# A quarter of two gradient stores moved to GpSimd's queue and spread unevenly over the DMA engines

## The chip, the cores and the metric

The kernel runs on one core of a Trainium2 chip. The core has a matrix engine (TensorE, "PE" in the profile, with its weight loads as "PEld"), VectorE ("DVE"), ScalarE ("ACT"), GpSimd ("POOL") and SyncE ("SP", which here only issues transfers). Transfers are carried out by 16 DMA engines. The metric is the device time of one execution in microseconds (us). The kernel before takes 638.99 us, the median of 3 runs (638.45 to 639.02).

## The reference

One query row per head attends to 8192 keys, for 32 heads of 128 columns, in bf16. The outputs are the attention result and the gradients of q, k and v for a given gradient of the output:

```python
scores = jnp.einsum('bhqd,bhkd->bhqk', q, k) * scale
attn = softmax(scores)
out = jnp.einsum('bhqk,bhkd->bhqd', attn, v)
# and the vjp of it: dq, dk, dv for grad_out
```

With one query row, dV is the outer product of attn and grad_out, and dK the outer product of the score gradient and q. K and V are read once (67 MB each) and dK and dV written once (67 MB each); everything else is small. K, V, dK and dV are [1, 32, 8192, 128].

## The kernel before

The 32 heads are taken as 16 pairs. A pair's K (or V, dK, dV) is a tile of 128 partitions with 128 rows of 128 bf16 numbers each, so 32 KB a partition and 4 MB in all. K tiles have 3 buffers, V tiles 2. `outer` writes dK and dV into the very tiles that held K and V, and the tiles are stored from there. A tile is worked on in 8 slices `r` of 16 rows (`NU` = 8).

Window j of the main loop (L328) does, for pair j, the scores from K, the softmax, the transposes of V (`v_transposes`, L202), the result (`contract` with "p") and dV (`outer`, L270); between them it finishes pair j-1: the score gradient, dQ (`contract` with "ds") and dK (`outer`, L270). The order of instructions on each engine is written out by hand (`tc.manual_schedule`), so what the program lists first is issued first.

All large transfers are issued from SP, in program order, and each of the 16 DMA engines works through its part of them in that order. In the steady windows SP issues, once each: the store of dK of pair j-1 (L278), the load of V of pair j+1 (`load_v`, L90, which waits until dV of pair j-1 has left that buffer), the store of dV of pair j (L278) and the load of K of pair j+2 (`load_k`, L84, which waits until dK of pair j-1 has left its buffer). Each is 4 MB in 128 packets of 32 KB, eight for each DMA engine. The first four pairs store in halves; the last pairs store in halves and quarters (`PARTS`), and the last V comes in quarters.

From window 6 on, `mark` (L104) issues one tiny load after each load of V or K, 15 in all: the n-th takes 4 bytes for each of n partitions into a small tile that nothing reads.

GpSimd does some memsets and the identity at the start, and nothing afterwards.

Of the kernel before, what the change touches and what calls it, by code (L numbers as in the profile page):

```python
# [11 lines left out]
BF16 = mybir.dt.bfloat16  # L12
# [10 lines left out]
K_BUFS = 3  # L23
V_BUFS = 2
QD = 32


@with_exitstack
def kernel(
# [11 lines left out]
    nc = tc.nc  # L41
    P = 128
# [4 lines left out]
    NT = 2 * S // P  # L47
    NU = NT // CH
    NQ = P // QD
    assert NU == 8 and NQ == 4  # L50
    W = D // 2
    NB = W // QD
    NG = NT // 4
# [3 lines left out]
    consts = ctx.enter_context(tc.tile_pool(name="consts", bufs=1))  # L57
# [12 lines left out]
    Kt, Vt, XK, XV, st, acc, qd = {}, {}, {}, {}, {}, {}, {}  # L70

    def rows_of(x, j, c=0, parts=1):
        L = NT // parts
        return x[0, 2 * j:2 * j + 2].rearrange("b s d -> (b s) d").rearrange("(p n) d -> p n d", p=P)[:, c * L:(c + 1) * L, :]

    def slots(X, c, parts):
        L = NT // parts
        return X[:, c * L:(c + 1) * L, :]

    def load_k(j):  # L80
        Kt[j] = kpool.tile([P, NT, D], BF16, tag="K", name="Kt")
        parts = 4 if j == 0 else 1
        for c in range(parts):
            nc.sync.dma_start(slots(Kt[j], c, parts), rows_of(k, j, c, parts))  # L84

    def load_v(j):
        Vt[j] = vpool.tile([P, NT, D], BF16, tag="V", name="Vt")
        parts = 4 if j in (0, HP - 1) else 1
        for c in range(parts):
            nc.sync.dma_start(slots(Vt[j], c, parts), rows_of(v, j, c, parts))  # L90
# [3 lines left out]
    nc.scalar.dma_start(rows[:, 1, :], grad_out.rearrange("b h s d -> (b h s) d"))  # L94
    load_k(0)
    load_v(0)
    load_k(1)
    load_v(1)
    load_k(2)

    marks = list(range(1, 16))
    marked = consts.tile([16, len(marks), 2], BF16)

    def mark():  # L104
        n = marks.pop(0)
        nc.sync.dma_start(marked[0:n, n - 1], k[0, 0].rearrange("(p n) d -> p n d", p=P)[0:n, 0, 0:2])

    ident = consts.tile([P, P], BF16)
    make_identity(nc, ident[:])
# [9 lines left out]
    nc.gpsimd.memset(q_win[:], 0.0)  # L119
    do_win = consts.tile([P, 2, 2, QD + 8], BF16)  # L120
    nc.gpsimd.memset(do_win[:], 0.0)
    wins = {}
    for which in ("p", "ds"):
        wins[which] = consts.tile([P, NG, QD], BF16, name=f"win_{which}")
        nc.gpsimd.memset(wins[which][:], 0.0)
# [3 lines left out]
    q_blk = consts.tile([P, HP, 2 * NB, NQ], BF16)  # L129
    four = small.tile([H, 2 * NB, NQ, QD], BF16, tag="S", name="four")  # L130
    for w in range(NB):
        for e2 in range(2):
            nc.scalar.copy(
                four[:, 2 * w + e2], rows[:, 0, :].rearrange("h (w j e) -> h w e j", w=NB, e=2)[:, w, e2:e2 + 1, :]
                .to_broadcast([H, NQ, QD]))
    tp = psT.tile([P, 2 * TB, P], BF16, tag="T", name="tp_q")
    for c in range(2 * NB):
        nc.tensor.transpose(tp[:, c, 0:H], four[:, c].rearrange("h a j -> h (a j)"), ident[0:H, 0:H])
    lane = consts.tile([P, QD], F32)
# [126 lines left out]
    def outer(j, which, r):  # L266
        x = st[j]
        G, dst = (Kt[j], out_2) if which == "dk" else (Vt[j], out_3)
        rep, row = x["ds"] if which == "dk" else x["p"], qd[j][:, 0 if which == "dk" else 1, :]
        nc.vector.tensor_tensor(  # L270
            slots(G, r, NU).rearrange("p n (a b) -> p n a b", b=R),
            slots(rep, r, NU).unsqueeze(2).to_broadcast([P, CH, D // R, R]),
            row.rearrange("p (a b) -> p a b", b=R).unsqueeze(1).to_broadcast([P, CH, D // R, R]),
            op=ALU.mult)
        parts = PARTS.get((which, j - HP), 2 if j < SPLIT else 1)
        if r % (NU // parts) == NU // parts - 1:
            c = r // (NU // parts)
            nc.sync.dma_start(rows_of(dst, j, c, parts), slots(G, c, parts))  # L278

# [48 lines left out]
    for j in range(HP + 1):  # L328
# [42 lines left out]
        if ends and j > 0:  # L371
            gather_copy("ds")
            if early:
                half(j, 0)
            for r in range(NU):
                outer(p_, "dk", r)
            if j + 1 < HP:
                load_v(j + 1)
# [9 lines left out]
        if not ends:  # L388
            gather_copy("ds")
            outer(p_, "dk", 0)  # L390
            outer(p_, "dk", 1)
# [44 lines left out]
        if not ends:  # L436
            for r in range(4, NU):
                outer(p_, "dk", r)
            if j + 1 < HP:
                load_v(j + 1)  # L440
                if j >= 6 and marks:
                    mark()
        for r in range(NU):
            if early:
                contract(j, "p", 4 * r, 4 * r + 4)
# [17 lines left out]
            do_window(j + 1)  # L463
        if 0 < j and j + 2 < HP:
            load_k(j + 2)
            if j >= 6 and marks:
                mark()

    result(dq_all, out_1)
    order.__exit__(None, None, None)  # L470
# [30 lines left out]
```

## Time and profile before

| | |
|---|---|
| median of 3 runs | 638.99 us (638.45 to 639.02) |
| the profiled execution | 638.61 us |
| its span, first to last instruction | 636.6 us |
| busy share of PE, DVE, ACT, POOL | 78%, 81%, 35%, 0% |
| bytes moved by DMA | 269.01 MB, 423 GB/s over the span |
| SP's queue ("q1"), share of 16 engines' time | 98.6% |

The table takes its numbers from the profile's page. The span is shorter than the time of its execution by 2.0 us, which lie before the first and after the last instruction. A queue's share says what part of the time of all 16 DMA engines its packets took. The trace has each packet's start, duration, size and queue, but not which of the 16 engines carried it.

### The profile page before, as it was taken

Reading aid. Unit: us, or ns where it says so; the run is one execution under the profiler, and the core shown is the slowest. Engines: PE = TensorE matmul, PEld = TensorE weight load, DVE = VectorE, ACT = ScalarE, POOL = GpSimd, SP = SyncE. Lnnn points to the kernel's source line nnn. Section 1 sums busy time; section 2 is a strip of 40 time slices with the busy share of each in tenths; the row PEclk is TensorE's granted clock in tenths of the full one; section 3 lists DMA queues with packets and bytes.
Section 4 is the critical chain, followed back from the end, with each engine's and each line's share of the span. In section 5 each row is a group of like instructions: output and inputs, shape, how many; then the busy total and the mean of one; then the engine's idle time right before and its main releaser. Section 6 shows DMA issues by size and latency. Waiting matters only on the chain.

```text
span 636.6 us, 8553 instructions
## 1 busy us (share of the span) xinstructions
PE 498.7 (78%) x3480; PEld 283.3 (44%) x3480; DVE 518.0 (81%) x654; ACT 221.8 (35%) x508; POOL 3.2 (0%) x10
## 2 busy tenths in 40 slices
PE   4787776888787987877978778887788877798771
PEld 1454443354453635444354453545436354363541
DVE  6589897979889798896789877798777987779882
ACT  2442434043342514335043340533405244152430
POOL 1000000000000000000000000000000000000000
PEclk9989899769798786979679797796977868779775
DMA  8999999999999999999999999999999999999995
GB/s 364 434 437 402 435 433 424 423 428 434 433 429 433 429 427 432 429 432 431 434 428 430 432 429 428 438 435 430 427 427 433 430 442 430 429 428 421 429 398 231
DMA packets 12854, 269.01 MB, mean 423 GB/s; under 512 B 1808, under 2 KB 1808, under 8 KB 1808
## 3 DMA queue, kind: packets, MB, share of 16 engines
q1 hardware_dynamic: 12720, 268.46, 98.6%
q8 instruction: 27, 0.44, 0.3%
q14 instruction: 11, 0.09, 0.0%
q10 hardware_dynamic: 96, 0.02, 0.0%
HBM read 134.23 MB, written 134.23 MB: 422 GB/s over the span
## 4 chain that ended last, share of the span: by engine, by line
PE 41%; DMA 26%; DVE 23%; ACT 4%; issue 3%; DVEq 0%; ACTq 0%; SPq 0%
DMA Kt<-in_k_dram 19%; PE s_ps L185 15%; PE T_ps L202 12%; DVE Kt L270 7%; DMA out_dram<-Kt 7%; DVE XK_sb L175 7%; PE acc_p L249 4%; PE acc_ds L249 4%; PE m_ps L262 3%; DVE Vt L270 3%; PE dp_ps L219 2%; ACT XV_sb L207 2%; DVE sT L192 1%; DVE dpT L230 1%; ACT p_rep L423 1%
## 5 line engine op out<-in xcount | busy, mean ns | idle before, releaser
L270 DVE TENSOR_TENSOR Vt<-p_rep,qd 128x2048 bf16<-128x2048 bf16 x128 | 155.4, 1225 | 55.2 <-PE acc_p L249 43.7
L185 PE MATMUL s_ps<-XK_sb,q_win 128*128 128x512 bf16 x512 | 152.3, 430 | 39.1 <-DVE XK_sb L175 33.6
L175 DVE STREAM_TRANSPOSE XK_sb<-Kt 128x1024 f32<-128x1024 f32 x128 | 151.3, 1221 | 21.1 <-PE s_ps L185 12.9
L207 ACT COPY XV_sb<-T_ps 128x512 f32<-128x512 f32 x256 | 139.9, 591 | 81.0 <-PE T_ps L202 80.9
L202 PE MATMUL T_ps<-ident_f,Vt 128*128 128x128 f32 x1024 | 167.2, 317 | 0.8 <-DMA Vt<-in_v_dram 0.8
L270 DVE TENSOR_TENSOR Kt<-ds_rep,qd 128x2048 bf16<-128x2048 bf16 x128 | 149.5, 1215 | 2.8 <-PE acc_ds L249 2.4
L202 PEld LDWEIGHTS T_ps<-ident_f,Vt 128*128 128x128 f32 x1024 | 133.7, 163 | 36.9 <-issue 20.5
L185 PEld LDWEIGHTS <-q_win 128*128 128x128 bf16 x512 | 51.5, 111 | 123.7 <-issue 92.1
L249 PE MATMUL acc_p<-Vt,win_p 128*32 128x512 bf16 x512 | 56.2, 441 | 3.3 <-ACT win_p L241 3.3
L249 PE MATMUL acc_ds<-Kt,win_ds 128*32 128x512 bf16 x512 | 42.5, 427 | 4.6 <-ACT win_ds L241 4.6
L219 PE MATMUL dp_ps<-XV_sb,do_win 128*32 128x512 bf16 x512 | 34.7, 386 | 13.5 <-ACT XV_sb L207 13.5
L255 ACT COPY S_ds<-acc_ds 128x512 f32<-128x512 f32 x16 | 9.4, 587 | 85.8 <-PE acc_ds L249 85.8
L241 ACT COPY win_ds<-ds 64x128 bf16<-64x128 bf16 x32 | 9.5, 296 | 75.6 <-DVE ds L300 75.4
L411 ACT ACTIVATE e<-sT,nbias 128x128 f32<-128x128 f32 x16 | 8.2, 515 | 69.7 <-DVE nbias L407 69.7
L262 PE MATMUL m_ps<-lane,S_ds 128*128 128x2 f32 x128 | 25.8, 324 | 4.1 <-DVE rinv L421 4.1
L219 PEld LDWEIGHTS <-do_win 128*32 128x32 bf16 x512 | 14.3, 94 | 29.3 <-issue 22.6
L262 PEld LDWEIGHTS m_ps<-lane,S_ds 128*128 128x128 f32 x128 | 24.4, 284 | 6.2 <-DVE rinv L421 5.2
L412 PE MATMUL m_ps<-rs,ones_f 128*128 128x1 f32 x32 | 8.0, 318 | 24.3 <-ACT e L411 24.3
L249 PEld LDWEIGHTS <-win_p 128*32 128x32 bf16 x512 | 13.4, 96 | 28.7 <-issue 25.5
L262 PEld LDWEIGHTS m_ps<-lane,S_p 128*128 128x128 f32 x128 | 21.4, 240 | 5.7 <-issue 2.3
L249 PEld LDWEIGHTS <-win_ds 128*32 128x32 bf16 x512 | 9.5, 100 | 32.0 <-issue 28.2
L398 PE MATMUL m_ps<-ident_f,top 128*128 128x128 f32 x16 | 4.8, 300 | 23.6 <-DVE top L396 23.6
(59 smaller groups left out, 201.3 us busy)
## 6 DMA issues: line engine op xcount, KB each, us to landing
Kt<-in_k_dram SPq DMA_DIRECT2D x15, 4096.0 KB
Vt<-in_v_dram SPq DMA_DIRECT2D x14, 4096.0 KB
out_dram<-Vt SPq DMA_DIRECT2D x11, 4096.0 KB
out_dram<-Kt SPq DMA_DIRECT2D x10, 4096.0 KB
out_dram<-Vt SPq DMA_DIRECT2D x10, 2048.0 KB
out_dram<-Kt SPq DMA_DIRECT2D x10, 2048.0 KB
Vt<-in_v_dram SPq DMA_DIRECT2D x8, 1024.0 KB
Kt<-in_k_dram SPq DMA_DIRECT2D x4, 1024.0 KB
```

Source lines behind the costliest of these rows:

```text
L175: nc.vector.transpose(XK[j, u][:].rearrange("p g w i -> p (g w i)"), slots(Kt[j], u, NU).rearrange("p g d -> p (g d)").bitcast(F32))
L185: nc.tensor.matmul(st[j]["s"][:], lhsT=q_win[:, c, at:at + P], rhs=cols[:, c // 2, c % 2], start=(u == 0 and c == 0), stop=(u == NU - 1 an ...
L202: nc.tensor.transpose(T_ps[:, i, :], words[:, m * P:(m + 1) * P], ident_f[:])
L207: nc.scalar.copy(XV[j][:, b * TB:(b + 1) * TB, :], st[j].pop(("T", c))[:])
L219: nc.tensor.matmul(out[b * QD:(b + 1) * QD, :], lhsT=do_win[:, b // 2, e2, at:at + QD], rhs=cols[:, z, e2, :, b * QD:(b + 1) * QD], start= ...
L241: nc.scalar.copy(wins[which][t * M:(t + 1) * M, :, 4 * t:4 * t + 4], src[t * M:(t + 1) * M])
L249: nc.tensor.matmul(acc[which][b * QD:(b + 1) * QD, :], lhsT=wins[which][:, g, :], rhs=X[:, 4 * g:4 * g + 4, :].rearrange("p n d -> p (n d) ...
L255: nc.scalar.copy(S[:].rearrange("p j d -> p (j d)"), acc.pop(which)[:])
L262: nc.tensor.matmul(bank[:, at:at + 2], lhsT=S[:, i, :], rhs=pick[:, i, 0:2], start=(i == 0), stop=(i == 3), skip_group_check=True)
L270: nc.vector.tensor_tensor(slots(G, r, NU).rearrange("p n (a b) -> p n a b", b=R), slots(rep, r, NU).unsqueeze(2).to_broadcast([P, CH, D // ...
L411: nc.scalar.activation(e[:].rearrange("p (u g) -> p u g", u=NU), x["sn"], ACT.Exp, bias=nbias[:], scale=scale, accum_out=rs[:])
L412: nc.tensor.matmul(x["m"][:, 0:1], lhsT=ones_f[:], rhs=rs[:], start=True, stop=True, skip_group_check=True)
```

## The change

The 15 marks are gone. For pairs 7 and 9 the store of dV is cut: SP stores the first three quarters of each partition's rows as soon as slice 5 is done, and GpSimd stores the last quarter (32 rows, 8 KB a partition, 1 MB in all) after slice 7. GpSimd does so with several transfers over groups of partitions, listed in `STEER` as (number of partitions, first DMA engine). The program assumes that a transfer over n partitions is spread over the largest divisor of n up to 16 engines, that these are consecutive, and that they start at a cursor which each transfer moves on by that number. `turn_to` moves the cursor to the wanted engine with a dummy load of as many partitions as the cursor must advance. These transfers are cut into packets of 4 KB (`max_dma_last_dim=4096`), and so is the load of V that stands in SP's queue ahead of them (pairs 8 and 10).

```diff
+SHARE = 4
+STEER = {
+    7: ((38, 15), (38, 7), (19, 2), (33, 5)),
+    9: ((98, 5), (30, 10)),
+}
     def load_v(j):
         Vt[j] = vpool.tile([P, NT, D], BF16, tag="V", name="Vt")
+        if j - 1 in STEER:
+            nc.sync.dma_start(Vt[j][:], rows_of(v, j), max_dma_last_dim=4096)
+            return
...
-    def mark():
-        n = marks.pop(0)
-        nc.sync.dma_start(marked[0:n, n - 1], k[0, 0].rearrange("(p n) d -> p n d", p=P)[0:n, 0, 0:2])
+    spare = list(range(8))
+    turned = consts.tile([16, len(spare), 2, 2], BF16)
+    cursor = [0]
+
+    def turn_to(lane):
+        n = (lane - cursor[0]) % 16
+        if n:
+            i = spare.pop()
+            nc.gpsimd.dma_start(turned[0:n, i], k[0, 0].rearrange("(p n) d -> p n d", p=P)[0:n, 0:2, 0:2])
+        cursor[0] = lane
+
+    def store_steered(dst, G, j):
+        a, c = 0, SHARE - 1
+        for n, lane in STEER[j]:
+            turn_to(lane)
+            nc.gpsimd.dma_start(rows_of(dst, j, c, SHARE)[a:a + n], slots(G, c, SHARE)[a:a + n], max_dma_last_dim=4096)
+            a += n
+            cursor[0] = (lane + max(m for m in range(1, 17) if n % m == 0)) % 16
+        assert a == P
+        if j == max(STEER):
+            turn_to(0)
...
-        if r % (NU // parts) == NU // parts - 1:
+        if which == "dv" and j in STEER:
+            L = NT - NT // SHARE
+            if r == NU - NU // SHARE - 1:
+                nc.sync.dma_start(rows_of(dst, j)[:, 0:L, :], G[:, 0:L, :])
+            elif r == NU - 1:
+                store_steered(dst, G, j)
+        elif r % (NU // parts) == NU // parts - 1:
...
-                if j >= 6 and marks:
-                    mark()
...
-            if j >= 6 and marks:
-                mark()
```

More of the change, by code (lines that the diff above doesn't have):

```diff
@@ L99 @@
     load_k(2)
-    marks = list(range(1, 16))
-    marked = consts.tile([16, len(marks), 2], BF16)
-    def mark():
-        n = marks.pop(0)
-        nc.sync.dma_start(marked[0:n, n - 1], k[0, 0].rearrange("(p n) d -> p n d", p=P)[0:n, 0, 0:2])
+    spare = list(range(8))
[17 more added lines that the diff above has]
+            turn_to(0)
     ident = consts.tile([P, P], BF16)
```

## The prediction

> **What bounds the kernel now.** I read the shares first, then the chain that ended last, SP's queue, and the end of the run. The page says that the DMA engines are full:
>
> ```profile
> DMA  8999999999999999999999999999999999999995
> DMA packets 12854, 269.01 MB, mean 423 GB/s; under 512 B 1808, under 2 KB 1808, under 8 KB 1808
> q1 hardware_dynamic: 12720, 268.46, 98.6%
> q8 instruction: 27, 0.44, 0.3%
> ```
>
> The digits are busy tenths of the 16 engines together; SP's queue alone takes 98.6% of them. In the chain, a load of K of 29 us is followed by compute and by a store of dK of 23 us, which frees the buffer for the next load:
>
> ```profile
> 349.20 29.35 DMA Kt<-in_k_dram
> ...
> 405.19 22.66 DMA out_dram<-Kt
> 427.89 29.35 DMA Kt<-in_k_dram
> ```
>
> 4 MB take an engine 8 packets of 1.213 us, 9.7 us; the other 13 to 20 us are the queue. So the loop runs at the pace of the DMA engines, and since a landing counts only when all 16 engines are through, of the slowest of them. The end shows that they are not alike (columns: stretch and length in us, four engines' and GpSimd's busy us, clock, DMA share, GB/s):
>
> ```profile
> 618.00:628.00 10.00, 3.92 (x18) 3.44 (x17) 5.98 (x6) 1.75 (x7) 0.00 (x0) 0.50 1.00 419
> 628.00:632.00 4.00, 0.00 (x0) 0.00 (x0) 0.00 (x0) 0.00 (x0) 0.00 (x0) 0.50 0.35 141
> 632.00:636.60 4.60, 0.00 (x0) 0.00 (x0) 0.00 (x0) 0.00 (x0) 0.00 (x0) 0.50 0.04 16
> ```
>
> After 628 us no compute is left and the engines drop out one by one; from 632 us on the share is 0.04, less than one engine of 16. The kernel waits for a single DMA engine.
>
> Which one, the packet records tell. On a busy engine one packet starts 3 ns before the last ends, so the packets fall into 16 chains. The marks number them: mark n leaves its 4-byte packets in n chains, each mark in one chain more than the one before. The lag of each engine behind the first, when the last 4 MB of dV and the next half of dK are through (605 us), and its end of data where that stands apart:
>
> ```
> engine   0   1   2   3   4    5   6   7   8   9   10  11  12  13  14  15
> lag us  0.0 2.0 0.1 7.0 10.8 4.3 3.8 0.0 0.1 7.6 6.2 4.8 4.6 3.9 4.0 0.1
> end us              631.7 634.9              632.3 630.9
> ```
>
> All carry the same bytes. Engines 0, 2, 7, 8 and 15 carry no instruction fetch (queues q8 and q14); the others get 3 to 6 each, a 16 KB one delaying its engine by about 1.4 us (0.95 for its packet, the rest on the data packet beside it), and engine 4's packets run slow by small amounts all along.
>
> **The change part by part.** Its core is rows per engine. A quarter of dV is 128 rows of 8 KB, 16 for each engine over the two pairs. By the divisors the diff counts on, 38 rows go to 2 engines, 19 to 1, 33 to 11, 98 to 14, 30 to 15, which makes
>
> ```
> engine       0  1  2  3  4  5  6  7  8  9 10 11 12 13 14 15
> rows after  28  9 28  2  2 12 12 31 31 10 12 12 12 12 12 31
> ```
>
> in place of 16 everywhere: most where the lag is 0, least on 3 and 4.
>
> Prices. Median packets take 1.213 us for 32 KB, 0.611 for 16 KB, 0.309 for 8 KB: about 8 ns fixed, the rest by bytes. A 4 KB packet then is (0.309+0.008)/2 = 0.1585 us, if nothing comes on top for alternating between two queues. Bounds for that extra: nothing or slightly less (ACT's 256-byte packets at the start ran between SP's at 15 to 18 ns, with SP's still at 309), and 0.34 us (a 16 KB instruction fetch took 0.95 against 0.611). I take nothing: ACT's is the row with a data queue.
>
> - Rows taken off: the 24 KB packets of the shorter store save 16 x 0.303 = 4.85 us on each engine. Rows put back: 0.317 us each (two packets).
> - V of pairs 8 and 10 in 4 KB packets: 64 x 0.1585 - 8 x 1.213 = 0.44 us, twice, 0.88 on each engine.
> - GpSimd issues 13 transfers (6 stores, 7 dummies); their completion packets, at most 15 ns each on an engine: 0.2 us. The dummies' 4-byte packets are in this.
> - Marks out: two 4-byte packets, about 13 ns each, on n engines: -0.3 us on engine 4 (11 marks), -0.15 on 9. On SP each took 0.3 us in a queue that waits anyway: nothing.
> - SP: the store of three quarters leaves two slices (2.6 us) earlier; SP waits for DVE there anyway, and the ring has 20 us of work ahead. Nothing.
> - GpSimd was idle after 4 us, so its own time costs nothing unless late (below). Order and counts on PE, DVE and ACT stay.
> - New wait: the load of V of pair 9 (and 11) waits for GpSimd's stores too; behind it in SP stand dV's store and the next K load. It was issued at 329.44 us, when the last engine had finished dV of pair 7, 328.9. Engines 7, 8 and 15 get 44 GpSimd packets beside the 64 of the V load, so the two alternate and end together, 7 us later there, at 321.9 us instead of 314.9; the three-quarter store gives 2.4 back, 329.2. Nothing. The transposes of V 8 start at 323.89, 2 us after that landing:
>
> ```profile
> 323.89 1.97 PE L202 MATMUL T_ps<-ident_f,Vt 128*128 128x128 f32 x8
> ```
>
> Sums, on the ends of data:
> engine 4: -4.85 + 0.63 + 0.88 + 0.2 - 0.3 = -3.4, from 634.9 to 631.5;
> engine 9: -4.85 + 3.17 + 0.88 + 0.2 - 0.15 = -0.75, from 632.3 to 631.6;
> engine 10: -0.1, 630.8; engine 3: 628.3;
> engines 7, 8, 15: without idling engine 0 would have ended at 632.3 - 7.6 = 624.7 (it idled 3.4 us for late issues); plus 9.83 - 4.85 + 0.88 + 0.2 = 6.1, so 630.8.
> The last end moves from 634.9 to 631.6 us, by 3.3. Compute follows: the last K load lands when engine 4 is through, lag 8.0 at 527 us; after the change the largest lag there is the 6.1 of 7, 8 and 15 (their part of the sum above), 1.9 us earlier, which is more than the last stores need, as engines 4 and 9 have work queued to the end. From the profiled 638.61 us that is 635.3. It lies 0.38 under the median and within the runs shown; from the median it would be 635.7. I say 635.5.
>
> The skill speaks against giving engines 7 and 15 the most: the Trainium skill, DMA: Bandwidth & Descriptors (Latency and other measured facts), calls them usually slower than the rest when GpSimd's descriptor rings are in use. In the trace of before, without such rings, they are among the fastest (lags 0.0 and 0.1); no row shows them with rings, and this is the second rival's mechanism.
>
> **The rivals.**
> *The rows land on other engines* (slower). The diff assumes spreading by divisor and a cursor at 0; no row shows a GpSimd transfer. If each is dealt out in equal shares over up to 16 engines from engine 0, 38 rows make 3 each, 19 make 2, 98 make 7: engines 0 to 8 get 20 rows, 13 to 15 get 9, 2 and 0. Engine 4: -4.85 + 6.34 + 0.8 = +2.3, end 637.2, time 640.9. It decides from 13 rows on engine 4, where the sum turns positive. The Trainium skill, DMA: Bandwidth & Descriptors (Why a DMA increments its semaphore), states both: the divisor with a round-robin cursor, and for some direct copies of GpSimd such equal shares. The marks, issued from SP, bear the diff's rule out below 16: their n rows went to n engines, always from the same one on. Above 16 no row tells the two apart.
>
> *GpSimd's packets cost more beside SP's.* Engines 7, 8, 15 carry 62 of them and have 634.9 - 630.8 = 4.1 us to lose: at 66 ns a packet the gain is gone, at 100 ns the time is 640.7.
>
> *The stores come late.* SP's V 9 load has until 343.5 us, when the engines run out of issued work. If GpSimd takes over 5 us for each transfer, the second store of 38 rows, third in its queue after 298.7 us, misses the V load, which is through at 315, and its packets alternate with 24 and 32 KB ones, about 1.1 us each; 38 of them end near 357 us, all engines idle some 14 us, time near 650. The Trainium skill, SBUF — State Buffer (the "DVE blocks DMA" trap), has a cause: DVE can lock GpSimd out while it writes descriptors. DVE is busy from 300.3 us, but in pieces of at most 1.25 us.
>
> *Nothing gained.* The fetches fall elsewhere: one more on 9 or 4 costs 1.4 us. Two more and the time is within 0.2%, 638.1.
>
> **How the numbers follow.** 0.2% (1.3 us) is about what a measurement here can tell from no change. Forecast 0.66, its own range 634.2 (one fetch fewer on each of 4 and 9) to 637.2 (one more). Other engines 0.12, packets 0.10 (a third of it within 0.2%), late 0.05, nothing gained 0.07. Faster 0.66, same 0.11, slower 0.23. To leave out no more than 2 in 10 the range goes up to the first rival's 640.9.
>
> **What would show it.** Right: the share after 632 us near zero and the span near 633.3; GpSimd's queue with 512 packets of 4 KB in about 20 us after 299 us; V 9 issued near 329 us, T_ps of V 8 without a wait; ends of engines within 3 us. Wrong: one engine alone draining at the end (rows misplaced), packets over 0.2 us (price), a hole in the DMA digits near 340 us (late).

## The result, and the profile after

The changed kernel takes 644.38 us (644.02 to 645.4) against 639.0 us (638.45 to 639.29): a ratio of 1.0088, with an interval of 1.007 to 1.0105. It is slower by 5.4 us, where 3.5 us less was forecast, and it lies above the range. The profiled execution took 644.35 us, its span is 642.4 us.

The page of the changed kernel, the lines on the DMA engines (digits and GB/s in 40 slices of the span, then packets and queues):

```profile
DMA  8999999999999999999997999999999999999996
GB/s 364 445 433 397 444 425 419 423 428 433 431 430 438 427 427 430 440 426 427 417 427 281 407 427 383 445 433 427 427 435 438 424 428 434 436 427 417 433 427 292
DMA packets 16934, 269.01 MB, mean 419 GB/s; under 512 B 3584, under 2 KB 3584, under 8 KB 6144
q1 hardware_dynamic: 14272, 266.36, 97.4%
q0 software_dynamic: 2528, 2.11, 1.0%
```

The digits were 9 from the second slice to the last but one; now there is a 7, in the slice that begins at 337 us, where GB/s falls to 281. GpSimd's queue, q0, holds 2528 packets. Only 512 of them are the expected 4 KB ones: the other 2016 have 4 or 8 bytes.

The stretch with the hole, by windows (columns as at the end of the kernel before: stretch and length, busy us of PE, PEld, DVE, ACT and POOL, clock, DMA share, GB/s):

```profile
342.00:346.00 4.00, 3.13 (x20) 2.02 (x20) 3.93 (x9) 0.59 (x2) 0.00 (x0) 1.00 0.84 331
346.00:350.00 4.00, 3.64 (x29) 1.24 (x29) 4.00 (x5) 0.16 (x1) 0.00 (x0) 1.00 0.26 82
350.00:354.00 4.00, 3.75 (x28) 0.95 (x25) 3.54 (x4) 0.58 (x1) 0.00 (x0) 1.00 0.80 264
634.00:638.00 4.00, 0.00 (x0) 0.00 (x0) 0.00 (x0) 0.00 (x0) 0.00 (x0) 0.50 0.80 333
638.00:642.40 4.40, 0.00 (x0) 0.00 (x0) 0.00 (x0) 0.00 (x0) 0.00 (x0) 0.50 0.07 29
```

In the three windows from 342 us the engines miss 4 x (0.16 + 0.74 + 0.20) = 4.4 us each on average; the kernel before had shares of 1.03, 1.01 and 1.00 there. The last two lines show what did come as forecast: the engines now end closer together. Their last packets of data end between 636.0 and 640.4 us, before between 628.0 and 634.8. But the mean moved from 629.6 to 637.5.

SP's part, from the timeline of the changed kernel (start, us, queue, line, transfer):

```profile
326.18 0.33 SPq L307 DMA_DIRECT2D out_dram<-Kt  x1
350.21 0.34 SPq L98 DMA_DIRECT2D Vt<-in_v_dram  x1
350.64 0.67 SPq L307 DMA_DIRECT2D out_dram<-Vt  x1
351.42 0.46 SPq L89 DMA_DIRECT2D Kt<-in_k_dram  x1
```

The group of SP's waits that this load belongs to (us in total, times, longest):

```profile
SPq L98 <- DMA out_dram<-Vt: 61.8, 11, 23.1
```

The load of V of pair 9 leaves at 350.21 us instead of 329.44. It waits 23.1 us for GpSimd's stores of dV of pair 7, and the next dV store and K load stand behind it. From 343 us on the engines run out of issued work. GpSimd itself was prompt, as the timeline of its engine shows:

```profile
302.58 1.02 POOL L124 DMA_DIRECT2D out_dram<-Vt  x1 [298.22 <-DVE Vt L293]
303.60 0.57 POOL L117 DMA_DIRECT2D turned<-in_k_dram  x1
304.16 1.02 POOL L124 DMA_DIRECT2D out_dram<-Vt  x1
...
307.34 0.63 POOL L124 DMA_DIRECT2D out_dram<-Vt  x1
307.97 0.58 POOL L117 DMA_DIRECT2D turned<-in_k_dram  x1
```

Its transfers take 0.56 to 1.03 us each to issue and the last has left at 308.6 us. They landed late. The DMA issues of the changed kernel, GpSimd's stores (size, median us from issue to landing):

```profile
out_dram<-Vt POOLq DMA_DIRECT2D x1, 784.0 KB, 20.2
out_dram<-Vt POOLq DMA_DIRECT2D x2, 304.0 KB, 30.1
out_dram<-Vt POOLq DMA_DIRECT2D x1, 264.0 KB, 42.7
out_dram<-Vt POOLq DMA_DIRECT2D x1, 240.0 KB, 20.6
out_dram<-Vt POOLq DMA_DIRECT2D x1, 152.0 KB, 43.8
```

The packet records say why. One rule accounts for all 2016 small packets: a GpSimd store of n rows over k engines gives each of those k engines 2n/k data packets, and each of the other 16 - k engines as many 4-byte packets, fillers. For the six stores that makes 38, 38, 38, 6, 14 and 4 packets on each of the 16 engines, 16 x 138 = 2208, of which 512 are data and 1696 fillers. With 16 completion packets for each of the 13 transfers (208) and 7 dummies of 16 packets of 8 bytes (112) the fillers make up the 2016. The same rule gives the totals of q0 in e2 (1280), e3 (416) and e6 (2112), though the trace does not name the engine of a packet. By it every engine has 120 packets of pair 7 in GpSimd's queue, whether it carries rows or not, and they go in order. Packets that start in each stretch of 5 us, all engines together, in the changed kernel:

```
from us                 305 310 315 320 325 330 335 340 345
q0, 4 KB                 20  41  36  10   8   9   7  34  91
q0, 4 bytes             180 400 242  86  69  58  66 271 420
SP, 4 KB (V of pair 8)  314 448 229   6   0   0   0   0   0
SP, 24 or 32 KB          19   1  45  80  68  65  65  54   6
```

Where both queues have work they take turns, one packet each (448 against 441 from 310 us). Beside the V load's 4 KB packets that is quick. From 320 us on the partners have 24 or 32 KB, and GpSimd's queue moves at their pace, 67 to 96 packets in 5 us, until SP has nothing left. The last of pair 7 starts at 349.27 us.

### The profile page after: what moved, and what is told of

Read it like the earlier page. It is cut to its first block, busy times and chain, and to the rows that moved or that the text cites. A ratio compares the mean times of both kernels' runs of the same rounds, so it can differ in the third digit from the quotient of the medians.

```text
span 642.4 us, 8557 instructions
## 1 busy us (share of the span) xinstructions
PE 496.7 (77%) x3480; PEld 283.4 (44%) x3480; DVE 518.3 (81%) x654; ACT 222.3 (35%) x508; POOL 12.2 (2%) x23
## 3 DMA queue, kind: packets, MB, share of 16 engines
q0 software_dynamic: 2528, 2.11, 1.0%
## 4 chain that ended last, share of the span: by engine, by line
PE 48%; DMA 23%; DVE 20%; ACT 4%; issue 2%; DVEq 0%; SPq 0%; ACTq 0%
PE s_ps L208 16%; DMA Kt<-in_k_dram 15%; PE T_ps L225 15%; DMA out_dram<-Kt 8%; DVE Kt L293 6%; DVE XK_sb L198 6%; PE acc_p L272 4%; PE acc_ds L272 4%; PE m_ps L285 4%; DVE Vt L293 3%; ACT XV_sb L230 2%; PE dp_ps L242 2%; DVE sT L215 1%; PE m_ps L441 1%; ACT e L440 1%
## 5 line engine op out<-in xcount | busy, mean ns | idle before, releaser
L225 PE MATMUL T_ps<-ident_f,Vt 128*128 128x128 f32 x1024 | 169.4, 319 | 6.6 <-DMA Vt<-in_v_dram 6.6
L225 PEld LDWEIGHTS T_ps<-ident_f,Vt 128*128 128x128 f32 x1024 | 136.2, 165 | 42.8 <-issue 27.5
L215 DVE STREAM_TRANSPOSE sT<-s_ps 128x512 f32<-128x512 f32 x16 | 11.5, 717 | 15.7 <-PE s_ps L208 15.7
```

Source lines behind the costliest of these rows:

```text
L215: nc.vector.transpose(sT[:].rearrange("p g r -> p (g r)"), x["s"][:])
L225: nc.tensor.transpose(T_ps[:, i, :], words[:, m * P:(m + 1) * P], ident_f[:])
```

## The experiments

Each is given against the kernel before, timed beside it. A ratio has its 95% interval. "Slow time" is what SP's packets between 295 and 610 us took above the median of their size, over all 16 engines; it is 15.6 us in the kernel before (instruction fetches mostly) and 58.8 in the changed one. Of these 58.8 us, 28.6 fall between 349.5 and 366 us, after the last GpSimd packet of pair 7 and before the first of pair 9: on all 16 engines the first 32 KB packet after the hole took 1.70 to 2.19 us, and a second round of such packets follows at 360.5 us. They belong to the hole and not to packets that stand beside GpSimd's.

### e1: the partners made small

```diff
-            nc.sync.dma_start(slots(Kt[j], c, parts), rows_of(k, j, c, parts))
+            nc.sync.dma_start(slots(Kt[j], c, parts), rows_of(k, j, c, parts), max_dma_last_dim=4096 if j == 9 else 65536)
...
-                nc.sync.dma_start(rows_of(dst, j)[:, 0:L, :], G[:, 0:L, :])
+                nc.sync.dma_start(rows_of(dst, j)[:, 0:L, :], G[:, 0:L, :], max_dma_last_dim=4096 if j == 7 else 65536)
```

> GpSimd's queue is left as in the changed kernel; on SP's queue the store of three quarters of dV of pair 7 and the load of K of pair 9 are cut into 4 KB packets too, so that 64 + 48 + 64 small packets stand beside GpSimd's 128 on each engine. Theory (filler: every engine carries about 128 GpSimd packets, most of them 4 bytes, which take turns one for one with SP's packets, so the last of the data waits behind 24 and 32 KB packets): GpSimd's stores of pair 7 end by about 337 us, the load of V of pair 9 is issued before 343 us, the hole after 343 us is gone, and the forecast's sum returns plus 0.8 us for the extra small packets: 636 to 637 us. Rival (GpSimd is late or locked out, or its path is dear in itself): the hole stays, 643 us or more.

641.34 us (638.04 to 644.21, twelve executions), 1.0043 [1.0027, 1.0058]. The load of V of pair 9 leaves at 336.28 us, no window has a hole, and GpSimd's stores of pair 7 land in 20.3 to 28.7 us. The windows of e1's profile:

```profile
342.00:346.00 4.00, 3.09 (x11) 1.63 (x11) 3.90 (x10) 0.00 (x0) 0.00 (x0) 0.65 0.97 418
346.00:350.00 4.00, 4.00 (x15) 2.57 (x14) 3.96 (x6) 0.70 (x3) 0.00 (x0) 0.50 1.01 434
350.00:354.00 4.00, 4.00 (x20) 0.94 (x22) 1.53 (x2) 0.06 (x1) 0.00 (x0) 0.57 1.01 434
628.00:632.00 4.00, 0.00 (x0) 0.00 (x0) 1.47 (x2) 0.00 (x0) 0.00 (x0) 0.50 1.01 422
632.00:636.10 4.10, 0.00 (x0) 0.00 (x0) 0.00 (x0) 0.00 (x0) 0.00 (x0) 0.50 0.41 164
```

Small partners remove the hole, and about 3 us with it. But the time is 4 to 5 us above the expected 636 to 637: the kernel stays slower than before, and its executions are 6 us apart. In the fastest, the one profiled, the largest lag of an engine is 6.1 us near 604 us (10.8 before), and all 16 end within 0.7 us, the lagging ones catching up while the others wait for the last stores, which SP issues from 622.68 us on (617.20 before).

### e2: the same rows, the fillers fewer

```diff
-    7: ((38, 15), (38, 7), (19, 2), (33, 5)),
+    7: ((38, 15), (90, 1)),
```

> Pair 7 is stored by two GpSimd transfers only, 38 rows on two engines and 90 on the 15 others: one engine gets 25 rows (50 data packets, more than the 44 of the changed kernel), but no engine gets more than about 52 GpSimd packets in all. Theory (filler): all of them fit beside the 64 packets of the V load, V of pair 9 is issued near 329 us, no hole; by rows engine 4 then ends at 633.3 us, 637.0 us in all. Rival (the concentration of data on a few engines makes the store late, not the filler): with 50 data packets on one engine the hole is there as before or deeper, 643 us or more.

640.99 us (639.21 to 642.36), 1.0031 [1.0021, 1.004]. Engine 0 takes 19 rows of pair 7 and engine 15 takes 25, which are 38 and 50 data packets in GpSimd's queue, but there are only 50 entries for each engine instead of 120. The load of V of pair 9 leaves at 329.78 us, as in the kernel before, and there is no hole (SP's timeline, and the queue's line):

```profile
329.78 0.34 SPq L98 DMA_DIRECT2D Vt<-in_v_dram  x1
q0 software_dynamic: 1280, 2.10, 0.9%
```

So 50 data packets on an engine are not the cause of the hole; the number of entries is, fillers included. The time, though, is 4 us above the expected 637.0.

### e3: pair 9 alone

```diff
-    7: ((38, 15), (38, 7), (19, 2), (33, 5)),
```

> Pair 7 is stored by SP as before, pair 9 as in the changed kernel (18 GpSimd packets on an engine). Theory (filler): no hole anywhere, GpSimd's two stores land in about 20 us, and engine 4 is relieved by 6 rows less one V load in small packets: 1.5 us faster than the kernel before, 637.0 us. Rival (GpSimd's path costs in itself): slower than the kernel before, above 640 us.

640.27 us (639.77 to 641.5), 1.0025 [1.0016, 1.0034]. Only 18 entries an engine, no hole (V of pair 9 at 330.07 us), and still slower, where 637.0 was expected; by its time alone this is the rival's side, which e5 tests. Its slow time is 27.2 us, with four packets of 32 KB between 2.1 and 3.6 us, beside pair 9's stores at 378 to 392 us; among the engines with such packets are, by their chains, 3 and 4, which carry only fillers of the 98-row store and two rows each of the other. They lost 3.5 and 1.9 us, as much as or more than the 1.9 us that the rows taken off gave each of them.

### e4: no GpSimd

```diff
             elif r == NU - 1:
-                store_steered(dst, G, j)
+                nc.sync.dma_start(rows_of(dst, j)[:, L:, :], G[:, L:, :])
```

> As the changed kernel, with the last quarters of dV of pairs 7 and 9 stored from SP in one transfer each, so nothing goes through GpSimd and all engines get the same bytes. Both theories: the small packets of two V loads cost 0.9 us, the marks taken out give 0.3 back, 639.2 us, no hole. If the V loads in small packets or the marks taken out were what slows the changed kernel, it would be 642 us or more.

639.77 us (639.05 to 640.44), 1.0016 [1.0007, 1.0024], slow time 19.8 us. The rows are spread evenly and no queue takes turns with SP's. What is left is the cut store, the marks' absence and the two V loads in 4 KB: 1.0 us more, against 0.88 - 0.3 = 0.6 in the sum.

### e5: GpSimd, spread evenly

```diff
-    7: ((38, 15), (38, 7), (19, 2), (33, 5)),
-    9: ((98, 5), (30, 10)),
+    7: ((128, 0),),
+    9: ((128, 0),),
```

> As the changed kernel, but each quarter is one GpSimd transfer of 128 rows over all 16 engines alike: 16 data packets on each engine, no filler packets, no uneven shares. Theory (the loss is filler: late stores, 124 more small packets on an engine, and SP's 32 KB packets slowed on the engines that get only filler): no hole, hardly any SP packet above 2 us after 300 us, and engine 4 as in the kernel with everything from SP: 639.5 to 640.0 us. Rival (GpSimd's path itself slows the engines): the slow packets of 380 to 392 us are there as in the kernel with pair 9 alone, 640.5 us or more.

639.87 us (638.9 to 641.21), 1.0018 [1.0008, 1.0027], not to be told from e4. Over 16 engines a store needs no filler: by the queue's line on the page q0 has 544 packets, 512 of data and 32 completions.

```profile
q0 software_dynamic: 544, 2.10, 0.8%
```

No 32 KB packet takes over 1.9 us, and the slow time is 21.6 us. 4 KB stores from GpSimd beside SP's packets cost nothing that can be told here; the uneven spreading costs, with the fillers, the dummies and the larger number of transfers that come with it.

### e6 and e7: small partners for one pair

```diff
# e6: as e1, with pair 7 alone
-    9: ((98, 5), (30, 10)),
# e7: as e3, and the store beside pair 9's quarter in 4 KB packets
-            nc.sync.dma_start(rows_of(dst, j, c, parts), slots(G, c, parts))
+            nc.sync.dma_start(rows_of(dst, j, c, parts), slots(G, c, parts), max_dma_last_dim=4096 if which == "dk" and j == 8 else 65536)
```

> The kernel of e1 (small packets beside all of pair 7's stores) without GpSimd's stores of pair 9. Theory (filler beside 32 KB packets slows SP's packets, beside small ones it does not): the slow packets of 380 to 392 us are gone, engine 4 keeps the relief of pair 7 alone (8 rows), and the time comes 1 us or so under that of e1 in its median, about 639 to 640 us. Rival (the scatter and the median of e1 come from pair 7): no change against e1, 641 us.

> Pair 9 alone through GpSimd, as in e3, but the store of dK of pair 8, which is on SP's queue while GpSimd's packets drain, is cut into 4 KB packets too. Theory (filler slows 32 KB packets beside it): the 12.5 engine-us of slow packets between 380 and 392 us shrink to under 4, engines 3 and 4 keep their relief of 6 rows, and the time is 1 to 2 us under e3: 638 to 639 us in spite of 0.4 us for the small packets. Rival (engines with filler alone are slowed whatever stands beside): slow packets as many as in e3, time 640.5 us or more.

e6: 639.03 us (638.1 to 640.28), 1.0006 [0.9997, 1.0015], no difference to the kernel before, and within the expectation: the best that the steering reached. e7: 641.19 us (640.6 to 641.46), 1.0035 [1.0021, 1.0049]. No packet of 32 KB takes over 1.9 us there any more (slow time 21.0 us against e3's 27.2), yet the time is no better than e3's. Small partners for pair 9 did not pay. The profile shows what the time followed in place of the slow packets. The last four stores leave 7.4 us later than in the kernel before (SP's timelines, the kernel before and e7):

```profile
617.20 7.14 SPq L278 DMA_DIRECT2D out_dram<-Kt  x4
624.64 7.14 SPq L306 DMA_DIRECT2D out_dram<-Kt  x4
```

From 624 to 628 us the share of the DMA engines is 0.68, and 15 of the 16 then end between 635.5 and 635.7 us: they had waited for these stores.

### e8: heavy engines without GpSimd

```diff
# the kernel before without marks; dV of pair 11: three quarters, then the last quarter
+                for n in (48, 69, 11):
+                    nc.sync.dma_start(rows_of(dst, j)[a:a + n, L:, :], G[a:a + n, L:, :])
+                    a += n
```

> The kernel before without its marks, no GpSimd transfer and no small packets; the last quarter of dV of pair 11 goes out from SP as 48 rows over 16 engines, 69 over three and 11 over eleven. If SP's transfers of 69 rows fall on engines 0 to 2, as the marks did, and bring no filler, engines 0 to 2 get 27 rows, 3 to 10 four, 11 to 15 three, instead of 8. The largest lag, engine 4's 10.8 us, falls by 1.2, and the marks give 0.3: 1 to 1.5 us faster than the kernel before, 637.3 us. If the compute chain and not the slowest engine set the end, no change: 638.7 us.

640.78 us (640.13 to 641.54), 1.0032 [1.0022, 1.0043]. From SP's queue an uneven store loses as well: the K load issued at 467.20 us takes 34.47 us to land in the chain of waits, where none after the first windows took more than 29.36 in the kernel before. The expected 637.3 is missed. This shows nothing of fillers; it shows that engines made heavy in the loop delay the loads that wait for all of them. It also shows slow packets without GpSimd: the slow time is 41.6 us, and among the 8 KB packets of the uneven store several took 0.88 to 1.45 us between 480 and 489 us, against a median of 0.309.

### e9 to e11: the last pair's dK not computed

e1's executions scatter by 6.2 us, the 13 of the kernel before beside e9 to e12 by 1.7. One explanation was a second bound: with engine 4 relieved, the compute of the last pair might set the end, and it is not the same in every run. In these three kernels the multiplications that write dK of the last pair are left out.

```diff
-        nc.vector.tensor_tensor(
+        if which == "dv" or j < HP - 1:
+            nc.vector.tensor_tensor(
```

> The kernel before, with the multiplications that write dK of the last pair left out (its stores then write what the K tile holds; 8 DVE instructions of 1.15 us, and the stores can go as soon as SP comes to them). Theory, two bounds: in the kernel before the end is set by the bytes of engine 4, whose queue hides the compute of the last pair, so the time stays, 638.2 to 639.0. Rival, compute alone sets the end: 9 us less compute, 634 or below.

> The kernel of e1_cover with the same multiplications of the last pair left out. Theory, two bounds: e1's executions scatter from 638.0 to 644.2 because the compute of the last pair, no longer hidden behind engine 4, sets when its fast engines get their last stores. Without it only the engines' bytes count: the prediction's 631.6 for the last end, 1.7 more for the small packets and 0.7 for more packets of 4 KB, 634.0, and 3.8 behind it: 637.8, at most 1 us apart between executions. Rival, the scatter comes from the DMA engines (slow packets beside GpSimd's): it stays, median above 640.5.

> The changed kernel with the same multiplications of the last pair left out. If the hole at 343 to 351 us costs DMA time that nothing gives back (8 us on an engine without lag, less on a lagging one), the engines still end late: 640 to 643. If the changed kernel's loss were only in the compute of the last pair, coming late: 638 as in e10.

e9: 638.73 us (638.21 to 639.33), 0.9996 [0.9987, 1.0005]: the kernel before doesn't wait for this compute, as expected. e10: 643.15 us (640.99 to 645.66), 1.0074 [1.0046, 1.0103]; e11: 645.77 us (644.18 to 648.12), 1.0105 [1.0079, 1.0131]. Neither is faster than its kernel with the compute; e10's expectation was wrong. The profile of e10 has no compute from 632 us on, and one engine ending at 636.9 us, 3.3 behind most.

### e12: GpSimd's stores in packets of 8 KB

```diff
-            nc.gpsimd.dma_start(..., max_dma_last_dim=4096)
+            nc.gpsimd.dma_start(..., max_dma_last_dim=8192)
```

> The changed kernel with GpSimd's stores in packets of 8 KB, so with half as many packets, data and filler, on every engine (about 64 for pair 7). Filler theory: those 64 pass beside the 64 packets of 4 KB of the V 8 load, before the 24 and 32 KB ones begin; no hole, V 9 issued by 333 us, 639.5 to 641.5. Rival, GpSimd's stores are late whatever their packets: V 9 stays at 350 us, time 644.

643.54 us (642.34 to 644.94), 1.0068 [1.0047, 1.0089]. The load of V of pair 9 leaves at 332.19 us, so the hole is gone as expected. But the time is 2 to 4 us above the expectation, and the queue's line shows another kernel than I had meant:

```profile
q0 software_dynamic: 640, 2.10, 0.9%
```

256 of the 640 are data, 208 completions and 112 dummies, which leaves 64 fillers. With one packet to a row the stores are not spread by divisor but in equal shares over 16 engines: 38 rows in shares of 3 leave 48 - 38 = 10 empty places, then 10, 19 in shares of 2 leave 13, 33 leave 15, 98 leave 14, 30 leave 2, together 64. This is the first rival's rule. Near 590 us the last engine lags 10.3 us behind the first, nearly as engine 4 did before, and one engine drains alone at the end (a share of 0.05 from 636 us on), until 638.2 us, where the first rival had put 637.2.

### e13 to e15: no compute before the end, and a second profile

e13 and e14 leave out the last pair's multiplications for dV too (`if j < HP - 1:` in the diff above), the one in the kernel before and the other in e1. e15 is e1's code.

> The kernel before with all 16 multiplications left out that write dV and dK of the last pair: their stores wait for the loads and SP's order only, so no compute stands before the end. Engine 4's bytes set the end: 638.2 to 639.1, the same as before. If compute had a part in it, 637.5 or less.

> The kernel of e1_cover with the same 16 multiplications left out. If the last pair's compute makes e1's scatter, this one gives 636 to 638 with executions at most 1.5 us apart. If bytes and slow packets on single DMA engines make it (e10's slowest engine ended at 637.0 us, 3.4 behind the first, with its queue never empty), it stays at 640.5 to 643.5 with a scatter of 3 us or more.

> The same code as e1_cover, for a second profile. If slow packets make the difference between executions, a profile above 640.5 us shows one or two engines ending over 2 us behind the others; if the last pair's compute does, all engines end within 1 us of each other as in e1, but later.

e13: 638.61 us (638.29 to 639.37), 0.9996 [0.9987, 1.0006]. e14: 642.18 us (637.98 to 644.5), 1.0043 [1.0023, 1.0063], with the scatter of e1. e15: 640.64 us, with one engine ending at 636.6 us, 1.3 behind the next and 2.7 or more behind twelve others. So neither the loss nor the scatter of e1's steering is the compute that writes the last pair's gradients. What differs most between these profiles is slow packets. GB/s beside GpSimd's stores and at the end, in e14's profile, one of 644.5 us:

```profile
324.00:330.00 6.00, 5.61 (x52) 3.86 (x52) 4.50 (x4) 3.54 (x7) 0.00 (x0) 0.82 1.01 364
386.00:392.00 6.00, 6.00 (x23) 3.09 (x25) 4.60 (x8) 0.75 (x3) 0.00 (x0) 0.50 0.96 355
...
632.00:636.00 4.00, 0.00 (x0) 0.00 (x0) 0.00 (x0) 0.00 (x0) 0.00 (x0) 0.50 0.40 164
636.00:642.50 6.50, 0.00 (x0) 0.00 (x0) 0.00 (x0) 0.00 (x0) 0.00 (x0) 0.50 0.05 19
```

and the same stretches in the kernel before:

```profile
324.00:330.00 6.00, 6.00 (x32) 4.39 (x32) 5.00 (x5) 3.21 (x7) 0.00 (x0) 0.55 1.00 431
386.00:392.00 6.00, 6.00 (x31) 2.28 (x32) 3.50 (x4) 0.16 (x1) 0.00 (x0) 0.60 0.99 426
```

The engines are as busy, but move 364 and 355 GB/s where they moved 431 and 426. Part of this comes with e1's small packets as such: e1's own, faster profile has 385 and 383 there. SP's 4 KB packets take up to 0.85 us there (0.159 at the median), its 32 KB packets up to 4.04 us. And a single engine is left at the end, with a share of 0.05. Over the profiles with e1's steering, one execution each, time goes with slow time:

```
                 slow time us   last data us   time us
kernel before        15.6          634.8        638.61
e1                   24.6          634.2        638.04
e15                  36.1          636.6        640.64
e10                  35.0          636.9        640.99
e14                  61.7          640.6        644.5
```

In each the time is 3.8 to 4.1 us behind the last packet of data. Between different steerings the order does not hold: e6's profile has a slow time of 30.3 us and a time of 639.06 us, e7's 21.0 and 641.46. What stands above the 15.6 us is beside GpSimd's stores but for one part of e14's: 16.2 of its 61.7 us fell at 462 to 478 us, with no GpSimd packet about.

### e16: the marks

```diff
-                if j >= 6 and marks:
-                    mark()
```

> The kernel before without the 15 marks and nothing else. By the prediction's sum 0.3 us less on engine 4: 638.3 to 638.9, not to be told from no change.

638.94 us (638.22 to 639.44), 0.9996 [0.9987, 1.0006]: the marks cost nothing that can be measured.

## Why the prediction was wrong

*What bounds the kernel.* Right for the kernel before. The time is set by its last DMA engine, and taking the last pair's writing compute out (e9, e13) changes nothing. Engine 4 was the one that held the end, and taking rows off it works: the largest lag near 604 us falls from 10.8 to 6.1 in e1, and the spread of the ends from 6.8 to 4.4 us in the changed kernel.

*Rows on the chosen engines.* Right for the changed kernel. The filler counts fit the divisors of the diff exactly, and as far as the packet chains can be followed, the engines without instruction fetches carry the many rows of pair 7. The first rival is refuted here, though its rule governs the stores with one packet to a row (e12). The Trainium skill, DMA: Bandwidth & Descriptors (Why a DMA increments its semaphore), has both rules, for different copies; the traces show both (1696 fillers by the divisors here, 64 by equal shares in e12).

*Prices of the data.* Right: GpSimd's 4 KB packets have a median of 0.159 us, forecast 0.1585, and V in 4 KB packets with the marks out measured +1.0 us [0.4, 1.5] where the sum had 0.6 (e4).

*"New wait: ... Nothing."* This is the first step that failed. It counted 44 GpSimd packets on engines 7, 8 and 15 beside the 64 of the V load and had both end together. There are 120 on every engine, nearly twice the V load's, so about half of them were still to come when SP's packets became 24 and 32 KB, and the load of V of pair 9 left at 350.21 us instead of 329.2. The hole takes 4.4 us from every engine on average. The third rival had this mechanism, turns with large packets at about 1.1 us each and a V load past 343.5 us; but its condition, over 5 us for each transfer on GpSimd, was not what brought it about (0.56 to 1.03 us). I gave it 0.05 because I tested it by the wrong quantity: when the stores are issued instead of how many packets each engine has to get through.

*"Completion packets at most 15 ns each ...: 0.2 us."* The second failed step, a mis-sized term. There are 126 small packets an engine instead of the few of 13 transfers; their records alone add up to 1.1 us on every engine.

*"I take nothing" for alternating.* The third. For an even store it holds (e5 against e4). For the steered stores the slow time rises by 9 to 46 us over the profiles with e1's steering, 0.6 to 2.9 us for each engine on average and more on single ones; without the part of e14's that has no GpSimd packet about, it is at most 1.9. In the changed kernel it rises by 43 us, but 27 of these are the packets after the hole. The second rival's break-even was 4.1 us on an engine; 1.1 of small packets and up to 1.9 of slow ones make 3.0 on average, and it is the unluckiest engine that counts. That the packets are slow because two queues alternate is not shown.

*The sum.* Put right with these terms, e1 comes near: the forecast end of 631.6 us, plus 0.9 more for small packets, 0.7 for the load and the store that e1 adds in 4 KB (0.44 as for V, and 8 x (6 x 0.1585 - 0.912) = 0.3), and for slow packets 0.6 (e1) or 1.3 (e15) as a mean over the engines gives 633.8 and 634.5; the profiles ended at 634.2 and 636.6. That e1's fits is in part luck: its 16 engines ended together because they had waited for the last stores, not because each was through with its bytes. In e14 the mean is 2.9, which gives 636.1, and the one last engine ended at 640.6: the slow packets do not fall evenly. For the changed kernel the hole's 4.4 and 2.7 of slow packets, 1.7 of them after the hole, come on top of 631.6 + 0.9, which makes 639.6; it ended at 640.4.

*"Compute follows."* Not tested by itself. In the changed kernel the last K load left at 553.52 us, 7.6 later than before, as the hole would have it, and the engines then had work to the end. But the step counted on the last stores leaving in time, and other profiles show that this is not given. From the issue of the last K load to the first of the last four stores it took 71.3 us in the kernel before and 70.3 in the changed one, at a granted TensorE clock of 0.91 from 575 to 612 us; at 0.72 it took 75.7 in e1, 76.1 in e7 and 76.0 in e16. In e16's profile 14 engines ended between 632.4 and 632.6 us, having waited for these stores (a DMA share of 0.79 from 612 to 624 us), and only a lagging engine, at 634.4, hid it. An end at 631.6 could not have been had in such an execution, whatever the packets cost. The clock as the cause is read from these profiles and not tested, and with the stores freed of the writing compute e10 and e14 were no faster.

*Nothing gained, and engines 7 and 15.* No fetch is needed to explain the loss. The Trainium skill's caution on engines 7 and 15 (DMA: Bandwidth & Descriptors, Latency and other measured facts) can't be weighed by these runs: the five engines without fetches, 7 and 15 among them, lag by 3.3 to 6.8 us in e1 at 433 us, but they had the most rows too.

*What stays open.* Why SP's packets take 2 to 4 us beside GpSimd's steered stores, and why one execution has 9 us of it and another 46. e5 shows that GpSimd's data packets alone don't do it, and e3 puts some of it on engines that carry mostly fillers; a store with fillers and no uneven data was not tried, so the two are not told apart. e8's uneven store from SP, e14's packets at 462 us and those after the hole show that packets can be slow without GpSimd.

## What to carry to other kernels

Before an uneven transfer is used to balance queues, count the packets that it puts on every engine, also on those that are to get none: in these traces, order within a queue and turns between queues made each of them as slow as its neighbour. Ask of a store whose buffer is waited for how many packets stand in its queue and what size their partners have, not when it is issued. And where the gain is a few us on one engine of 16, a cost of a few us that falls on any engine by chance takes it back: look at the scatter as well as the median.

## What the runs showed of the hardware

- A GpSimd store that uses k of the 16 engines, with two packets to a row, puts a 4-byte packet on each of the others for every data packet of one engine that it uses: 1696 fillers for six stores with 512 data packets, and none when all 16 engines are used (e5). This is the rule by which the counts of four kernels come out.
- With one 8 KB packet to a row the same stores went in equal shares over all 16 engines, with 64 fillers (e12).
- Two queues with work on one engine took turns by packets, whatever their size: 67 to 96 packets of GpSimd's in 5 us beside 65 to 80 of 24 or 32 KB.
- SP's packets beside steered stores took up to 0.89 us for 4 KB and up to 4.04 us for 32 KB, against medians of 0.159 and 1.213 (e1, e14).
- Without a GpSimd packet about, the first 32 KB packets after the idle stretch took 1.70 to 2.19 us on all 16 engines (changed kernel, from 351.2 us), and 8 KB packets of an uneven store from SP up to 1.45 us against a median of 0.309 (e8).
- The time from the last K load to the last stores went with the granted clock from 575 to 612 us: 70.3 and 71.3 us at 0.91, 75.7 to 76.1 at 0.72.
